# Attention before experts on one core: masks moved to TensorE, transposes two pairs ahead, banded heads first with one output tile per head, one v transfer, dummy matmuls

## Chip, cores and metric

The kernel runs on one core of one Trainium2 chip. The metric is the device time of one execution in microseconds (us), as the median over several executions. A "fast" execution is one within 1.5% of the fastest of its kernel; only those enter the ratios. The executions were spread over several chips, and the kernel before takes 277 to 282 us on the first of them and 267 to 271 us on the later ones, so kernels are compared by ratios or with runs beside them on the same chip.

## The reference

Four batches of attention with 8 heads, 768 positions and head size 64. Heads 0, 2 and 6 are causal ("retrieval"); heads 1, 3, 4, 5 and 7 are "streaming": they see the first 4 positions (the sinks) and the last 64. Every token then goes to one of 8 experts (two-layer networks, 512 to 1024 to 512), chosen by a given domain number.

```
scores = scale * q @ k.T
mask   = causal                                  for retrieval heads
mask   = causal & (pos < 4 | distance < 64)      for streaming heads
a      = softmax(where(mask, scores, -1e9));  x = a @ v     # all heads joined: 3072 x 512
out[domain == e] = relu(x[domain == e] @ w1[e]) @ w2[e]     # e = 0..7
```

## The kernel before

Work is in float16 with float32 sums in PSUM. For each batch and pair of heads, q and k are transposed on TensorE, copied out, multiplied into scores, passed through exp on ScalarE, and masked on VectorE by multiplying with 0 and 1. The product with v carries a column of ones (65 columns), which gives the softmax's denominator.

The masking on VectorE (cut):

```
# causal heads: after exp, the diagonal blocks are multiplied by the 0/1 mask
nc.vector.tensor_tensor(out=d, in0=d, in1=m_diag..., op=ALU.mult)
# streaming heads: the whole band is multiplied by the 0/1 mask
nc.vector.tensor_tensor(out=et, in0=et, in1=m_str..., op=ALU.mult)
```

The product with v of the streaming heads: one output tile holds all five heads of one block `it` of 128 positions; one sink product for all heads, 330 columns wide, and then ten band products, two for each head:

```
def part(it):                                   # six of these a batch
    ps = av_pool.tile([P, 5, VW], FP32, ...)
    if it > 0:
        nc.tensor.matmul(out=ps[all five heads],                  # 330 columns
            lhsT=eSink[b][0:96, P*(it-1) : P*it],                 # stationary 96 x 128
            rhs=vs_sink[0:96, b, :, :], start=True, stop=False)
    for h, s in SIDX.items():                                     # five heads
        for a in (2*it, 2*it + 1):
            nc.tensor.matmul(out=ps[hp : hp+64, s, 0 : D+1],
                lhsT=et[:, 64*a : 64*a + 64],                     # stationary 128 x 64
                rhs=rhs[:, 0 : D+1], ...)
    # ... normalize on VectorE, scatter the 128 rows to the experts' slots
```

After the last batch the kernel loads the tokens of expert 0 back (`load_x`), transposes them and runs the experts:

```
load_x(0); load_x(1)
x_transpose(0)
load_w(wB, 3)              # the fourth of the experts' weights
for e in range(E):
    layer1(e); ...; layer2(e); ...
```

The softmax here doesn't subtract the row's maximum and nothing guards it: scores larger than these inputs give would overflow.

## Time and profile before

| | before |
|---|---|
| median of 3 runs | 277.36 us (277.27 to 279.59) |
| profiled span | 275.1 us, granted TensorE clock 0.83 |
| attention: first scores to last matmul | 14.5 to 138.1 us |
| first expert matmul | 157.4 us |
| experts and output | to the end, TensorE full |

First the page of the profile: busy microseconds by engine with the share of the span, and the clock granted to TensorE in tenths of full speed in 40 equal slices of the span ("9" is 0.9 or more).

```profile
PE 196.7 (72%) x1979; PEld 109.9 (40%) x1979; DVE 120.9 (44%) x340; ACT 92.5 (34%) x109; POOL 120.8 (44%) x191
...
PEclk9999999655696558855955569999999999999995
```

Next the busy time of each engine by stretches of 15 us; the first columns are the stretch and its length, the last three the granted clock, the DMA share and GB/s.

```profile
core 0: us, PE busy (x) PEld busy (x) DVE busy (x) ACT busy (x) POOL busy (x), PEclk, DMA share, GB/s
...
75.00:90.00 15.00, 11.65 (x190) 7.11 (x190) 14.22 (x51) 9.31 (x11) 5.60 (x8) 0.81 1.53 169
...
120.00:135.00 15.00, 9.92 (x196) 7.19 (x190) 10.21 (x29) 5.45 (x7) 4.05 (x7) 0.60 0.11 37
135.00:150.00 15.00, 1.78 (x33) 1.00 (x33) 3.31 (x13) 0.00 (x0) 9.19 (x16) 0.63 0.46 102
```

The clock reads 9 in the first slices (before 46.6 us the trace has no record of it), but that is no measurement, and so the mean of 0.83 is too high: two causal score products of 448 columns take 0.56 us there at 42 us, and 0.36 us at 105 us, so TensorE ran cold early on. No engine is full in attention. In 75 to 90 us VectorE comes near it (14.22 of 15); from 135 to 150 hardly anything runs on TensorE. The list of waits says what TensorE stood still for: waiting instruction, the event that released it, us in total, times, longest.

```profile
engine line waited for: us in total, times, longest us
PE tpx_0_2304 L715 <- DMA xe_2297<-x_slots: 16.8, 1, 16.8
PE dom_ps L488 <- DVE r_dlow L484: 8.3, 1, 8.3
PE scs_2_0_453 L301 <- DVE kT_2_439 L218: 6.2, 1, 6.2
PE scs_2_0_946 L301 <- DVE kT_2_932 L218: 5.3, 1, 5.3
PE scs_2_0_1490 L301 <- DVE kT_2_1461 L218: 3.1, 1, 3.1
```

The largest wait is between attention and experts, for the tokens of expert 0 (`xe`). Many of the others are for VectorE, which copies the transposed k (`kT`) late because it is busy with masks. Last, the timeline of TensorE in one block of the streaming heads: start, duration, line, output and inputs, stationary tile (rows x columns), moving tile. Durations overlap, because matmuls are pipelined; the differences of the starts are what counts.

```profile
133.69 0.30 PE L419 MATMUL avs_1_2171<-vs_sink,eSk_2075 96*128 96x330 f16 x1 [0.43 <-DVE rcps_0_2163 L443]
133.92 0.22 PE L435 MATMUL avs_1_2171<-vsh_1793,eS_3_3_2015 128*64 128x65 f16 x1
133.92 0.22 PE L435 MATMUL avs_1_2171<-ve_1097,eS_3_3_2015 128*64 128x65 f16 x1
133.97 0.20 PE L435 MATMUL avs_1_2171<-vsh_1793,eS_3_2_1950 128*64 128x65 f16 x1
...
134.07 0.19 PE L435 MATMUL avs_1_2171<-ve_1097,eS_3_1903 128*64 128x65 f16 x1
134.35 0.31 PE L419 MATMUL avs_2_2191<-vs_sink,eSk_2075 96*128 96x330 f16 x1
```

### The profile page before, as it was taken

To read this page: it belongs to the slowest core of one execution; us is meant where nothing else is said; L and a number is where in the kernel's file an instruction comes from. 1 tells how busy PE (TensorE), PEld (TensorE's weight loads), DVE (VectorE), ACT (ScalarE), POOL (GpSimd) and SP (SyncE) were. 2 spreads that over 40 slices of the span, in tenths; PEclk is the share of its full clock that TensorE was granted. 3 is DMA by queue.
4 is the path that set the end of the run, shared out by engine and by line. 5 is a ranking of instruction groups with operands and counts; after the bars stand their busy time and mean duration, and the time that the engine had idled before them with its cause. 6 is when DMAs were issued, how large, how long until landed. Compare 5 with 4: busy or idle time off the path is not lost. (4 is left out here: it accounts for less than half of the span.)

```text
span 275.1 us, 4932 instructions
## 1 busy us (share of the span) xinstructions
PE 196.7 (72%) x1979; PEld 109.9 (40%) x1979; DVE 120.9 (44%) x340; ACT 92.5 (34%) x109; POOL 120.8 (44%) x191
## 2 busy tenths in 40 slices
PE   0279178783578478757600399999999999999940
PEld 0235045352344255444500245544554545454410
DVE  0835953874799654976720103141413141413120
ACT  1186067333585158625000032404150505051400
POOL 8579398584725840242464001535344440504140
PEclk9999999655696558855955569999999999999995
DMA  7999999957999549510119999899999998202030
GB/s 134 236 172 137 182 60 170 155 98 141 193 203 138 97 85 187 95 60 19 50 70 168 239 230 224 206 213 270 213 276 229 272 229 215 112 4 92 17 112 1
DMA packets 55731, 41.27 MB, mean 150 GB/s; under 512 B 27901, under 2 KB 49301, under 8 KB 55703
## 3 DMA queue, kind: packets, MB, share of 16 engines
q0 software_dynamic: 50096, 35.67, 78.9%
q1 hardware_dynamic: 5606, 5.24, 6.9%
q8 instruction: 16, 0.26, 0.4%
q14 instruction: 13, 0.10, 0.1%
HBM read 56.64 MB, written 11.53 MB: 248 GB/s over the span
## 5 line engine op out<-in xcount | busy, mean ns | idle before, releaser
L400 POOL DMA_INDIRECT x_slots<-xb_1111,dest_i x6 | 6.7, 1122 | 23.1 <-DVE xb_1111 L451 20.9
L177 POOL DMA_DIRECT2D ve_1097<-in_v_dram x12 | 9.0, 772 | 10.0 <-DMA w_0_943<-in_moe_w_dram 3.7
L715 PE MATMUL tpx_0_2304<-ct,xe_2297 128*128 128x128 f16 x8 | 1.0, 311 | 16.8 <-DMA xe_2297<-x_slots 16.8
L177 POOL DMA_DIRECT2D ve_159<-in_v_dram x12 | 9.3, 804 | 4.8 <-DMA k_156<-in_k_dram 3.1
L177 POOL DMA_DIRECT2D ve_141<-in_v_dram x12 | 9.0, 762 | 4.9 <-DMA q_131<-in_q_dram 2.6
L749 POOL DMA_INDIRECT out_dram<-ob_2404,idx_i x1 | 1.0, 1049 | 22.8 <-DVE ob_2404 L748 22.8
L742 ACT ACTIVATE hT_2329<-h_0_0_2330 128x896 f16<-128x896 f32 x1 | 0.9, 917 | 30.0 <-PE h_0_0_2330 L735 30.0
L177 POOL DMA_DIRECT2D ve_600<-in_v_dram x12 | 8.9, 772 | 4.4 <-DMA k_597<-in_k_dram 3.1
L400 POOL DMA_INDIRECT x_slots<-xb_1633,dest_i x6 | 5.8, 972 | 6.4 <-DVE rcps_1_2183 L443 3.4
L715 PEld LDWEIGHTS <-xe_2297 128*128 128x128 f16 (+1 forms) x16 | 1.4, 138 | 17.1 <-DMA xe_2297<-x_slots 16.9
L400 POOL DMA_INDIRECT x_slots<-xb_614,dest_i x6 | 6.5, 1083 | 3.0 <-DVE xb_614 L451 1.8
L400 POOL DMA_INDIRECT x_slots<-xb_245,dest_i x6 | 6.1, 1024 | 1.5 <-issue 1.1
L719 DVE COPY xT_2303<-tpx_0_2304 128x1024 f16<-128x1024 f16 x1 | 0.7, 691 | 13.4 <-PE tpx_0_2304 L715 13.4
L488 PE MATMUL dom_ps<-ct,r_dlow 24*128 24x24 f16 x1 | 0.2, 197 | 8.3 <-DVE r_dlow L484 8.3
L735 PEld LDWEIGHTS <-w_0_941 128*128 128x128 f16 x32 | 3.8, 119 | 5.4 <-issue 3.8
L301 PE MATMUL scs_2_0_453<-qT_2_388,kT_2_439 64*64 64x128 f16 (+2 forms) x12 | 0.5, 311 | 6.2 <-DVE kT_2_439 L218 6.2
L719 DVE COPY xT_2370<-tpx_0_2371 128x1024 f16<-128x1024 f16 x1 | 0.7, 692 | 9.3 <-PE tpx_0_2371 L715 9.3
L749 POOL DMA_INDIRECT out_dram<-ob_3152,idx_i x1 | 1.0, 971 | 7.8 <-DVE ob_3152 L748 7.8
L749 POOL DMA_INDIRECT out_dram<-ob_3021,idx_i x1 | 1.0, 971 | 7.7 <-DVE ob_3021 L748 7.7
L735 PEld LDWEIGHTS <-w_1_1485 128*128 128x128 f16 x32 | 3.1, 98 | 3.0
L735 PEld LDWEIGHTS <-w_5_2578 128*128 128x128 f16 x32 | 3.1, 98 | 3.0
L735 PEld LDWEIGHTS <-w_7_2831 128*128 128x128 f16 x32 | 3.1, 98 | 3.0
(875 smaller groups left out, 650.8 us busy)
## 6 DMA issues: line engine op xcount, KB each, us to landing
x_slots<-zt SPq DMA_DIRECT2D x8, 128.0 KB, 8.0
w_0_941<-in_moe_w_dram POOLq DMA_DIRECT2D x1, 1024.0 KB
w_0_943<-in_moe_w_dram POOLq DMA_DIRECT2D x1, 1024.0 KB
w_1_1485<-in_moe_w_dram POOLq DMA_DIRECT2D x1, 1024.0 KB
w_1_1487<-in_moe_w_dram POOLq DMA_DIRECT2D x1, 1024.0 KB
w_2_2271<-in_moe_w_dram POOLq DMA_DIRECT2D x1, 1024.0 KB
w_2_2273<-in_moe_w_dram POOLq DMA_DIRECT2D x1, 1024.0 KB
w_3_2325<-in_moe_w_dram POOLq DMA_DIRECT2D x1, 1024.0 KB
```

The source lines that it names most:

```text
L177: nc.gpsimd.dma_start(out=ves[b][:, t, 4 * par : 4 * par + 4, 0:D], in_=v[b, par::2, t * P : (t + 1) * P, :].rearrange("h p d -> p h d"),)
L301: yield lambda g=g, a0=a0, a1=a1, hp=hp: nc.tensor.matmul(out=dst[hp : hp + 64, a0 - c0 : a1 - c0], lhsT=kT[b, pi][rows, 64 * g : 64 * g + ...
L400: ins = nc.gpsimd.indirect_dma_start(out=xs_dram, out_offset=bass.IndirectOffsetOnAxis(ap=dest_i[:, t : t + 1], axis=0), in_=xbs[b][:, it, :],
L488: nc.tensor.transpose(out=dps[:], in_=dlow[:], identity=ident[0:NT, 0:NT])
L715: nc.tensor.transpose(out=ps[:, j, c, 0:n], in_=xe[e][0:n, g, c * P : (c + 1) * P], identity=ident[0:n, 0:n])
L719: nc.vector.tensor_copy(out=xT[e][:, :, 0:256].rearrange("p c (j n) -> p c j n", j=2), in_=ps[:].rearrange("p j c n -> p c j n"),)
L735: nc.tensor.matmul(out=sc[:, j, 0:CAP], lhsT=w1t[:, c, ft * P : (ft + 1) * P], rhs=xT[e][:, c, :], start=(c == 0), stop=(c == 3),)
L742: nc.scalar.activation(out=hT[e][:, 2 * fp : 2 * fp + 2, :], in_=sc[:, :, 0:CAP], func=AF.Relu)
L749: ins = nc.gpsimd.indirect_dma_start(out=out, out_offset=bass.IndirectOffsetOnAxis(ap=idx_i[:, col : col + 1], axis=0), in_=ob[:], in_offs ...
```

## The change

Its intent is to free VectorE, and to keep TensorE from waiting for it. The masks become additive and are matmuls with the identity, summed into the scores in PSUM before exp. The transposes of q and k run two head pairs ahead. The banded (streaming) pairs come first in a batch, and their products with v fill the gaps of the causal pairs. Each streaming head gets its own output tile for all six blocks, so that it can be normalized at once. v of a batch is one transfer. Dummy matmuls at the start and before the experts are to warm the clock. Parts of the routing arithmetic are rewritten. The core of the diff (cut, marked by "# ..."):

```diff
-PAIRS = [(0, 2), (6, 7), (1, 3), (4, 5)]
+PAIRS = [(1, 3), (4, 5), (6, 7), (0, 2)]
-    c16[:, 128:256] = pp[:, None] <= pp[None, :]
+    c16[:, 128:256] = np.where(pp[:, None] <= pp[None, :], 0.0, NEG)
# ... causal heads: score pieces are cut at the diagonal block, which gets a mask
+                mb = lambda c0=c0, c1=c1: nc.tensor.matmul(
+                    out=dst[:, c0 - p0 : c1 - p0], lhsT=ident, rhs=m_diag, start=False, stop=True
+                )
-            for J in range(NSO):
-                if 448 * c <= OFF[J] < 448 * c + 448:
-                    d = et[:, :, OFF[J] : OFF[J] + P]
-                    nc.vector.tensor_tensor(
-                        out=d, in0=d, in1=m_diag.unsqueeze(1).to_broadcast([P, 2, P]), op=ALU.mult
-                    )
# ... streaming heads: the mask is the first product of each half
+    def str_bias(c, dst):
+        nc.tensor.matmul(
+            out=dst[:, 0:384], lhsT=ident, rhs=m_str[:, 384 * c : 384 * c + 384], start=True, stop=False
+        )
# ... the product with v of the streaming heads: one tile for each head
-    def a_str_units(b):
-        def part(it):
-            # one sink product of 330 columns, then ten band products
+    def a_str_units(b, h):
+        def part(t0):
+            def f():
+                if t0 == 0:
+                    st["ps"] = av_pool.tile([P, NSO, VW], FP32, tag="av", name=f"avs_{b}_{h}")
+                for it in (t0, t0 + 1):
+                    if it > 0:
+                        nc.tensor.matmul(
+                            out=ps[:, it, 0 : D + 1],
+                            lhsT=eSink[b][0:96, P * (it - 1) : P * it],
+                            rhs=vs_sink[0:96, b, s, 0 : D + 1],
+                            start=True,
+                            stop=False,
+                        )
+                    for a in (2 * it, 2 * it + 1):
+                        kk = 64 if a == 0 else P
+                        nc.tensor.matmul(
+                            out=ps[hp : hp + 64, it, 0 : D + 1],
+                            lhsT=et[0:kk, 64 * a : 64 * a + 64],
+                            rhs=rhs[0:kk, 0 : D + 1],
+                            start=(it == 0),
+                            stop=True,
+                        )
+                if t0 == NSO - 2:
+                    normalize(b, h, ps)
# ...
+    def warm(n, name):
+        ps = sc_pool.tile([P, 2, 512], FP32, tag="sc", name=f"warm_{name}")
+        for i in range(n):
+            nc.tensor.matmul(out=ps[:, i % 2, :], lhsT=zt[:, 0:P], rhs=zt[:], start=True, stop=True)
# ... load_v: 12 transfers become one; scatters come after the last head of a batch
# ... stages of a batch: streaming pairs, sinks, causal pair, head 6; transposes two pairs ahead
     load_x(0)
     load_x(1)
+    warm(16, "moe")
     x_transpose(0)
     load_w(wB, 3)
```

The sink product was one for all heads of a block, and is now one for each head and block. In the order of the program it stands directly before that head's two band products: a stationary tile of 96 x 128, two of 128 x 64, again 96 x 128, and so on.

## The prediction

> **What bounds it now.** The busy table by stretches shows three parts of the 275.1 us span. Attention ends on TensorE at 138.1. Until the first expert matmul at 157.4 (timeline) nothing computes: scatters leave GpSimd until 143.8, the first x load is issued at 145.5, and TensorE waits 16.8 us for it (list of waits) while weights 2 and 3 share the DMA engines. Then the experts: TensorE busy 15.0 of every 15 us until 265, and the output tail.
>
> Attention takes 31 us a batch: first scores at 14.5, 42.4, 75.1, 105.2. TensorE is busy 86.3 of 127 us, VectorE 85.6, ScalarE 61.7. TensorE's waits on VectorE sum to about 30 us after the start: kT copies (6.2, 5.3, 3.1, 2.4, four of 1.9), mask products and normalizations. The gaps also cool the clock: granted clock 0.63 to 0.74; a 64x448 score matmul takes 550 ns in batches 0 and 1, 360 in 2 and 3. The Trainium skill ("TensorE: Matmul & The Clock Gate", Part 1) says that about 3.4 us of idling halves the clock; these pairs agree.
>
> **What the change does.**
> - Removes VectorE mask products: 6.4+4.1+8.9+2.2 = 21.6 us, some 8 us more of routing and kbd copies (3.9, to GpSimd).
> - Adds to TensorE per batch 18 masks of 128 columns, 10 of 384, about 15 cuts, 20 sink products: an estimate of 4 us, at the measured 50 to 60 ns per small matmul.
> - Transposes two pairs ahead take the 0.95 us kT copies out of TensorE's way: most of the 30 us of waits go, TensorE stays warm. Estimate: 20 to 23 us a batch.
> - Start: transposes at about 8 us instead of 10.9. But in batch 0 kbd copies sit behind the second v transfer in GpSimd's order, which waits until the first v has landed, near 25.5 (q and k of batch 1 land at 29.4 and 33.3). Stall of about 5 us at the sink scores, until 26 to 28.
> - One v transfer saves GpSimd 7 us a batch, off the path; rows stay 64 elements, so DMA time stays: 16 us a batch (q, k 3.9 each, v 8). With 11 to 12.5 us per expert's weights, loads up to weights 2 keep the DMA queue busy until about 110: nearly a second bound.
> - All six scatters now come after the last head, 1.28 us each: about 3 us more.
> - Dummy matmuls before the experts end long before x lands; the first expert still starts cold (572 ns matmuls). Worth about 0.
>
> **Sum.** Attention ends near 26.5 + 14 + 3x21.5 = 105 to 108 instead of 138. Normalization and scatters 9, load issue 1.6, x landing 7 to 9.5, transposes 2.5: first expert matmul near 129 instead of 157.4. Experts and tail unchanged (118 us). Gain 28 us.
>
> Predicted: **249 us**, 8 in 10 between 239 and 262. Faster by over 2%: 0.96; within: 0.02; slower: 0.02.
>
> **What shows each step.** First scores spaced 20 to 23 us from batch 1 on; TensorE's waits on VectorE in attention under 10 us; score matmuls of 360 ns from batch 1; a wait at batch 0's sink scores until 26 to 28; 19 to 23 us between attention's last matmul and the first expert's; expert stretch still full; first expert matmuls near 570 ns.
>
> **What would make it wrong.** The DMA queue is the bound: weights 2 delay the last scatters (255 to 262). TensorE, with more and smaller matmuls, needs 26 us a batch (262). Or x lands faster, with only weights 3 beside it, and the dummies bridge the gap (238).

## More of the kernel before

The five pairs of band products start within 0.15 us of each other, from 133.92 to 134.07. From the last pair to the next sink product it takes 0.28 us, of which TensorE is shown idle for 0.09.

## The result, and the profile after

| | before | changed |
|---|---|---|
| median, same chip | 278.48 us (277.27 to 282.2, 4 runs, the last one slow) | 296.98 us (295.82 to 297.72, 4 runs) |
| ratio of fast runs | | 1.068 (95%: 1.060 to 1.076) |
| profiled span, granted clock | 275.1 us, 0.83 | 294.9 us, 0.78 |
| attention's last matmul ends | 138.1 us | 154.4 us |
| first expert matmul | 157.4 us | 177.2 us |

A ratio is the mean time of one kernel's fast runs over that of the other's fast runs of the same rounds, so it is not quite the ratio of the medians quoted. The kernel became slower by about 7% where 10% faster was predicted. All of it lies before the experts: after the first expert matmul both kernels need 118 us.

The page of the changed kernel, the same lines as before:

```profile
PE 249.6 (85%) x2248; PEld 137.2 (47%) x2248; DVE 92.6 (31%) x208; ACT 93.2 (32%) x109; POOL 97.7 (33%) x167
...
PEclk9795555695559855596559556999999999999995
```

VectorE has lost 28 us of busy time, as intended. TensorE has gained 53, of which 36 in attention (122.2 against 85.8). The stretches show how full it is, and at what clock:

```profile
core 0: us, PE busy (x) PEld busy (x) DVE busy (x) ACT busy (x) POOL busy (x), PEclk, DMA share, GB/s
...
30.00:45.00 15.00, 15.00 (x128) 8.64 (x127) 3.87 (x11) 4.14 (x6) 1.52 (x1) 0.50 1.87 182
...
105.00:120.00 15.00, 15.00 (x143) 8.77 (x142) 5.31 (x20) 6.76 (x8) 0.36 (x2) 0.50 0.81 137
```

TensorE is shown busy for 15.00 of 15.00 us, and yet its granted clock is 0.50, as if it idled. VectorE is at 3.87 of 15. The list of waits confirms that TensorE no longer waits for VectorE:

```profile
PE tpx_0_2411 L724 <- DMA xe_2387<-x_slots: 16.2, 1, 16.2
PE sck_421 L364 <- POOL kbd L223: 7.4, 1, 7.4
PE tpk_0_183 L204 <- DMA k_132<-in_k_dram: 2.4, 1, 2.4
PE avs_4_1601 L442 <- DVE xb_1315 L383: 1.4, 1, 1.4
```

So the waits that the change was to remove are gone, and TensorE spends longer than before on what it executes. The timeline of one streaming head says on what:

```profile
29.89 0.23 PE L431 MATMUL avs_1_443<-vs_sink,eSk_420 96*128 96x65 f16 x1
30.05 0.26 PE L442 MATMUL avs_1_443<-vsh_429,eS_0_0_255 128*64 128x65 f16 x1
30.06 0.26 PE L442 MATMUL avs_1_443<-ve_141,eS_0_0_255 128*64 128x65 f16 x1
30.25 0.23 PE L431 MATMUL avs_1_443<-vs_sink,eSk_420 96*128 96x65 f16 x1
30.41 0.26 PE L442 MATMUL avs_1_443<-vsh_429,eS_0_0_255 128*64 128x65 f16 x1
30.42 0.26 PE L442 MATMUL avs_1_443<-ve_141,eS_0_0_255 128*64 128x65 f16 x1
30.61 0.23 PE L431 MATMUL avs_1_443<-vs_sink,eSk_420 96*128 96x65 f16 x1
```

A group of three small products (the sink product and two band products) takes 0.36 us, from 29.89 to 30.25 and from 30.25 to 30.61, at a clock near 0.50. Elsewhere, at a higher clock (64 to 66 us), it still takes 0.29 us. The two band products start 0.01 us apart. The time passes between the tile of 128 columns and the tiles of 64 columns, in both directions. No line shows a wait (a wait would stand in brackets). Together the sink and band products keep TensorE busy for 43.2 us in the changed kernel, against 16.6 us before (overlaps counted once).

The Trainium skill has a sentence for this. The page "TensorEngine Tiling (Array Packing)", section "Key Properties" under "Tiling Modes", says that changing the tiling mode, "not just tile", drains TensorE. It gives no cost. The modes that the page lists are tile sizes: 128 x 128, 128 x 64, 64 x 128 and so on. Here the mode is taken to be the size class of the stationary tile, which the probe below bears out. Counting the changes of this class along the matmul records of attention, one by one, gives 173 before and 411 in the changed kernel (96 rows counted as 128, which the probe below justifies).

**Theory A.** Every change of tiling mode costs a fixed drain. The change adds more than 200 of them, mostly by alternating sink and band products, some by the mask matmuls. If the array does no work while it drains, the clock falls too, though the profile shows TensorE busy.

**Rival B.** The sink product and the band products sum into the same PSUM words directly after one another, and the accumulation waits for the write. The number of switches would then not matter, and writing other words in between would help.

**Other rivals.** The mask matmuls alone cost it; or the dummy matmuls do.

### The profile page after: what moved, and what is told of

Its sections match the earlier page's. It is cut to its first block, busy times and chain, and to the rows that moved or that the text cites. A ratio compares the mean times of both kernels' runs of the same rounds, so it can differ in the third digit from the quotient of the medians.

```text
span 294.9 us, 5270 instructions
## 1 busy us (share of the span) xinstructions
PE 249.6 (85%) x2248; PEld 137.2 (47%) x2248; DVE 92.6 (31%) x208; ACT 93.2 (32%) x109; POOL 97.7 (33%) x167
## 5 line engine op out<-in xcount | busy, mean ns | idle before, releaser
L457 POOL DMA_INDIRECT x_slots<-xb_1847,dest_i x6 | 6.0, 1000 | 17.7 <-DVE xb_1847 L383 16.5
L252 PEld LDWEIGHTS <-ct 128*128 128x128 f16 x72 | 5.6, 106 | 11.6 <-issue 10.7
L758 POOL DMA_INDIRECT out_dram<-ob_2511,idx_i x1 | 1.1, 1054 | 25.0 <-DVE ob_2511 L757 25.0
L364 PE MATMUL sck_421<-qT_0_181,kbd 128*32 128x320 f16 x2 | 0.9, 448 | 7.4 <-POOL kbd L223 7.4
L457 POOL DMA_INDIRECT x_slots<-xb_254,dest_i x6 | 6.4, 1071 | 2.2 <-DVE r_olo L495 1.3
L728 DVE COPY xT_2410<-tpx_0_2411 128x1024 f16<-128x1024 f16 x1 | 0.7, 693 | 20.5 <-PE tpx_0_2411 L724 20.5
L457 POOL DMA_INDIRECT x_slots<-xb_1315,dest_i x6 | 6.0, 1003 | 2.1 <-DVE xb_1315 L383 1.2
L457 POOL DMA_INDIRECT x_slots<-xb_748,dest_i x6 | 6.0, 1002 | 2.1 <-DVE xb_748 L383 1.2
L744 PEld LDWEIGHTS <-w_0_1201 128*128 128x128 f16 x32 | 3.8, 120 | 5.6 <-issue 4.3
L481 PEld LDWEIGHTS <-zt 128*128 128x128 f16 x29 | 3.3, 122 | 6.0 <-issue 3.4
L223 POOL COPY kbd<-kT_0_638 64x4 f16<-64x4 f16 x2 | 0.4, 212 | 16.9 <-DVE kT_0_638 L217 16.9
L481 PE MATMUL warm_start<-zt 128*128 128x512 f16 x10 | 4.2, 600 | 1.3 <-DVE zt L623 1.3
L223 POOL COPY kbd<-kT_0_1756 64x4 f16<-64x4 f16 x2 | 0.4, 182 | 13.0 <-DVE kT_0_1756 L217 12.9
L364 PEld LDWEIGHTS <-kbd 128*32 128x32 f16 x24 | 0.7, 96 | 8.3 <-POOL kbd L223 8.0
L744 PEld LDWEIGHTS <-w_5_2685 128*128 128x128 f16 x32 | 3.1, 98 | 3.0
L744 PEld LDWEIGHTS <-w_7_2938 128*128 128x128 f16 x32 | 3.1, 98 | 3.0
L744 PEld LDWEIGHTS <-w_1_1660 128*128 128x128 f16 x32 | 3.1, 98 | 3.0
L744 PEld LDWEIGHTS <-w_3_2432 128*128 128x128 f16 x32 | 3.1, 98 | 3.0
L744 PEld LDWEIGHTS <-w_2_2001 128*128 128x128 f16 x32 | 3.0, 98 | 3.2 <-issue 0.4
```

Source lines behind the costliest of these rows:

```text
L223: nc.gpsimd.tensor_copy(out=kbd[r, b % 2, g, 4 * hh : 4 * hh + 4], in_=dst[r, 0:4])
L252: mb = lambda c0=c0, c1=c1: nc.tensor.matmul(out=dst[:, c0 - p0 : c1 - p0], lhsT=ident, rhs=m_diag, start=False, stop=True)
L364: nc.tensor.matmul(out=sc[32 * g : 32 * g + 32, c, 0:320], lhsT=kbd[:, b % 2, g, :], rhs=qT[b, PAIRS.index(pr)][:, P + 320 * c : P + 320 * ...
L457: ins = nc.gpsimd.indirect_dma_start(out=xs_dram, out_offset=bass.IndirectOffsetOnAxis(ap=dest_i[:, t : t + 1], axis=0), in_=xbs[b][:, it, :],
L481: nc.tensor.matmul(out=ps[:, i % 2, :], lhsT=zt[:, 0:P], rhs=zt[:], start=True, stop=True)
L728: nc.vector.tensor_copy(out=xT[e][:, :, 0:256].rearrange("p c (j n) -> p c j n", j=2), in_=ps[:].rearrange("p j c n -> p c j n"),)
```

## The experiments

### One pattern at a time: probe

This kernel computes nothing of the reference and gives a wrong result (it writes zeros). It runs bursts of 65-column products after a stretch of large matmuls that warm the clock: tiles of 128 columns only; pairs of 64-column tiles only; the two alternating on the same PSUM words, then on other words; grouped by fives; two halves in place of the full tile; 64 rows against 128; and 96 rows against 128.

```diff
+    def p_alt_same(ps, rows=96, shift=0):      # shift=3: other PSUM words
+        for i in range(60):
+            full(ps, (i + shift) % 6, rows=rows, start=(i == 0))
+            for hp in (0, 64):
+                half(ps, i % 6, hp, stop=(i == n - 1))
```

> A kernel of matmul patterns alone (wrong result on purpose), 60 groups each of 65 columns, after a burst that keeps the clock at full rate. Theory A: only 128-column tiles, 50 to 60 ns a matmul; only pairs of 64-column tiles, 60 to 70 ns a pair; 128-column matmul and pair in turn, 280 to 300 ns a group, the same with 96 or 128 rows and whether the pair adds to the same words or to others; with the 128-column matmul cut in two halves, under 150 ns a group; five and five, under 170 ns a group. Theory B: in turn but to other words, under 170 ns a group; halves, still near 280.

The windows of the probe, one for each pattern (60 repetitions each): 128 columns only; pairs only; alternating, its first 5.5 us; the rest of it; grouped by fives; 96 against 128 rows.

```profile
core 0: us, PE busy (x) PEld busy (x) DVE busy (x) POOL busy (x), PEclk, DMA share, GB/s
20.16:21.98 1.82, 1.82 (x62) 1.82 (x61) 0.00 (x0) 0.00 (x0) 1.00 0.03 9
27.25:29.27 2.02, 2.02 (x121) 1.98 (x121) 0.00 (x0) 0.00 (x0) 1.00 0.04 8
34.46:40.00 5.54, 5.54 (x59) 3.89 (x57) 0.00 (x0) 0.00 (x0) 0.99 0.01 3
40.00:54.66 14.66, 14.66 (x123) 9.36 (x123) 0.00 (x0) 0.00 (x0) 0.50 0.00 1
...
128.34:134.77 6.43, 6.43 (x181) 5.30 (x180) 0.00 (x0) 0.00 (x0) 1.00 0.01 3
...
165.82:169.72 3.90, 3.90 (x121) 3.90 (x120) 0.00 (x0) 0.00 (x0) 1.00 0.00 0
```

A full tile alone takes 30 ns (1.82 us over 60), a pair alone 34 ns (2.02 over 60), so a group of both without a switch would take 64 ns. Alternating at clock 0.99, the full tiles start 287 ns apart in the trace. Each group has two switches, so one switch costs (287 - 64) / 2, or about 111 ns. Grouped by fives, 60 groups with 24 switches took 6.43 us, 107 ns a group: (107 - 64) x 60 / 24 = 108 ns a switch. The two patterns agree; 0.108 us is used below. After the clock has fallen to 0.50 a group takes 360 ns. If the 64 ns of work double there to 128, a switch takes 116 ns: its length hardly depends on the clock.

Other results of the same run: alternating on other PSUM words took 340 ns a group over the whole burst, on the same words 337 (287 and 360 ns at the two clocks in both), so Rival B is refuted here. With two halves in place of the full tile a group took 82 ns, a burst with no switch (with a gap of 0.70 us at its issue). A tile of 64 rows against one of 128, both with 128 columns, took 309 ns a couple (at a mean clock of 0.65; 270 at full clock), so rows are part of the mode. Rows of 96 against 128 took 65 ns a couple (3.90 us over 60), so these are one mode.

The other half of the theory is in the third and fourth lines. The pattern is the same, TensorE is shown busy all the time, and the clock falls from 0.99 to 0.50 after 5.5 us. It fell in each of the four bursts that alternate shapes (one of them with a full tile of 128 rows), 4.0 to 5.6 us after their start, and in none of the others. Three of these lasted under 4 us, but the one by fives lasted 6.4. The Trainium skill ("TensorE: Matmul & The Clock Gate", Part 1) says that the gate follows how busy the array has been over windows of about 3.4 us. That agrees only if drains count as idle, which no view of the profile shows as such.

### Fewer switches, other switches: e1_hoist, e2_stagger, e3_dvemasks

The first computes the five sink products of a head first, then its band products. The switches fall, and the products remain.

```diff
+                # ... sink(i) is the sink product of block i; start and stop flags are moved to match
+                if t0 == 0:
+                    for i in range(1, NSO):
+                        sink(i)
                 for it in (t0, t0 + 1):
-                    if it > 0:
-                        nc.tensor.matmul(...)      # the sink product of this block
```

> The changed kernel, with the five sink products of each banded head issued first and its banded products after them; same number of matmuls, same operands. Theory A (the array loses about 0.1 to 0.15 us at each change between 128-column and 64-column stationary tiles): 8 changes fewer per head, 160 in all, so a head's products fall from 1.7 to 2.2 us to about 1 us, and the kernel from 297 to 272 to 280 us. Theory B (a matmul that adds to the PSUM words just written must wait for that write): much the same gain, since the distance grows too. Theory C (the added mask matmuls are the cause): within 1% of the changed kernel.

Measured: 259.7 us, ratio 0.962 (0.954 to 0.970). By moving 100 small products the kernel went from slower to faster than the one before. Expected were 272 to 280 us. Against the changed kernel on a chip like this one (294.59 us, below) it gained 35 us, of which 176 fewer switches make 19; the granted clock in attention rose besides, from 0.61 to 0.79.

The second issues the sink product of the next block before the bands of this one. It has nearly as many switches as the changed kernel (383 against 411), but the products that follow one another write other PSUM words.

```diff
                 # ... sink(i) and the flags as above
                 for it in (t0, t0 + 1):
-                    if it > 0:
-                        nc.tensor.matmul(...)      # the sink product of this block
+                    if it + 1 < NSO:
+                        sink(it + 1)
```

> The changed kernel, with the sink product of block it+1 issued just before the banded products of block it: as many changes between 128- and 64-column tiles as before, but never two matmuls in a row into the same PSUM words. Theory A: within 1% of the changed kernel (297 us), 0.29 to 0.36 us per block still. Theory B: as fast as the run with the sinks hoisted (272 to 280 us).

Measured: 292.06 us, ratio 1.081 (1.071 to 1.091). It is as slow as the changed kernel, within 0.9% (294.59 us on a like chip, below). Rival B falls in the kernel as well as in the probe.

The third puts all masks back on VectorE as 0/1 products after exp, and leaves the alternation.

```diff
-                mb = lambda c0=c0, c1=c1: nc.tensor.matmul(out=..., lhsT=ident, rhs=m_diag, ...)
+                    nc.vector.tensor_tensor(out=d, in0=d, in1=m_diag..., op=ALU.mult)
     # ... the mask tables hold 0 and 1 again; streaming heads:
-            str_bias(c, sc[:, 0, :])
+            nc.vector.tensor_tensor(out=et, in0=et, in1=m_str..., op=ALU.mult)
```

> The changed kernel with the masks as products on VectorE again, everything else kept. Theory A: about 90 changes of the tile shape fewer and 72 + 40 mask matmuls fewer, 12 to 18 us of TensorE time, of which waits on VectorE give back a few: 280 to 288 us. Theory C (the masks are the whole cause): 265 us or less.

Measured: 283.28 us, ratio 1.052 (1.043 to 1.061). The masks on TensorE cost something here (11 us against the changed kernel's 294.59), but taking them away leaves the kernel slower than before. They are not the main cause.

### The alternation alone, in the kernel before: b1_alternate

Only the sink product of the kernel before is split into one for each head, each directly before its band products. Masks, transposes and order stay.

```diff
-                if it > 0:
-                    nc.tensor.matmul(out=ps[all five heads], ..., rhs=vs_sink[0:96, b, :, :], ...)
                 for h, s in SIDX.items():
+                    if it > 0:
+                        nc.tensor.matmul(out=ps[:, s, :], ..., rhs=vs_sink[0:96, b, s, :], ...)
```

> The kernel before, with only this part of the change: the sink product of a block, one matmul of 330 columns for five heads, becomes five of 65 columns, each just before the banded products of its head. 80 matmuls more; 160 changes more between 128- and 64-column tiles. Theory A, with 0.11 us per change as the matmul patterns showed: 17 us, and a few more by a cooler clock: 6 to 9% slower than the kernel before. If only the count of matmuls matters (30 to 60 ns each): 1 to 2% slower.

Measured: 283.75 us against 268.82 for the kernel before beside it, ratio 1.059 (1.050 to 1.067). That is 15 us for 160 switches (333 against 173 in the traces) and 80 small products more. At 0.108 us a switch alone 17 us were to be expected if every one lay on the critical path.

### The sink product in two halves: e5_halves, e6_halves_k128

Here the order stays as the change has it, and only the shape changes. The sink product is cut into two with 64 columns each. That is 100 products more, and no switch between sinks and bands.

```diff
                     if it > 0:
-                        nc.tensor.matmul(out=ps[:, it, 0 : D + 1],
-                            lhsT=eSink[b][0:96, P * (it - 1) : P * it], ...)
+                        for hp in (0, 64):
+                            nc.tensor.matmul(out=ps[hp : hp + 64, it, 0 : D + 1],
+                                lhsT=eSink[b][0:96, P * (it - 1) + hp : P * (it - 1) + hp + 64], ...)
```

> The changed kernel, with each sink product cut into two 64-column halves in its old place, between the banded products: 100 matmuls more than the changed kernel, and no change of tile shape between sinks and bands. Theory A: as fast as the run with hoisted sinks (0.96 of the kernel before) or up to 1% faster. If the count of matmuls, or writes to the same words, were the cause: slower than the changed kernel (over 1.07).

Measured: 261.77 us (one of four runs slow), ratio 0.972 (0.960 to 0.985). That is faster than the kernel before, but whether by 2% is unclear. With 100 products more than the changed kernel it is far below its ratio of 1.07 to 1.09, so neither the number of products nor the writes to the same words are the cause.

The next also lets the first band product of each head contract 128 rows rather than 64 (the added rows contribute zeros), so no switch is left between the products with v of a head.

```diff
-                        kk = 64 if a == 0 else P
+                        kk = P
```

> The same, and the first band product of a head contracts over 128 rows (the added rows are zero) instead of 64, so that a head has no change of shape at all: 40 changes fewer. Theory A: 4 to 5 us faster than the run with halves alone, about 0.945 of the kernel before.

Measured: 248.01 us (two of four runs slow; the fast ones took 245.5 and 246.46), ratio 0.925 (0.913 to 0.936); it beats both kernels. The timeline shows the same work as the three lines of the changed kernel's groups, now in one mode:

```profile
55.62 0.19 PE L443 MATMUL avs<-vsh,eS 128*64 128x65 f16 x1
55.62 0.19 PE L443 MATMUL avs<-ve,eS 128*64 128x65 f16 x1
55.65 0.20 PE L432 MATMUL avs<-vs_sink,eSk 96*64 96x65 f16 x2
55.69 0.20 PE L443 MATMUL avs<-vsh,eS 128*64 128x65 f16 x1
```

A group of two sink halves and two bands now takes 0.07 us (from 55.62 to 55.69), where three products took 0.29 to 0.36. The sink scores of the four batches start at 26.7, 48.2, 70.9 and 91.2 us, 20 to 23 us apart, which is the spacing that the prediction gave for the changed kernel.

From the one edit to the other 32 switches go (223 to 191 in the traces; 40 were expected), about 3.5 us, but the time falls by 14. The windows of attention explain it, from the first sink scores to the last matmul (columns as above). First the halves alone:

```profile
26.80:117.20 90.40, 86.73 (x1470) 54.45 (x1471) 49.02 (x120) 54.78 (x67) 36.49 (x66) 0.77 1.07 147
```

Then the halves with 128 rows:

```profile
26.70:104.00 77.30, 72.82 (x1506) 47.34 (x1507) 49.10 (x122) 55.58 (x67) 36.49 (x66) 0.95 1.27 175
```

And the changed kernel:

```profile
27.10:154.40 127.30, 122.21 (x1406) 73.72 (x1407) 49.61 (x122) 55.70 (x67) 36.83 (x66) 0.63 0.85 117
```

The granted clock is 0.77, 0.95 and 0.63. An account in two terms, an estimate worked out from the traces, fits these five kernels: the length of a drain is fixed, and the rest of the busy time is work that stretches with the clock. The work at full clock is then clock x (busy - switches x 0.108 us).

| kernel | switches | clock | PE busy, us | of it drains, us | work at full clock, us |
|---|---|---|---|---|---|
| changed | 411 | 0.63 | 122.2 | 44.4 | 49.0 |
| e2_stagger | 383 | 0.61 | 120.2 | 41.4 | 48.1 |
| e1_hoist | 235 | 0.79 | 86.7 | 25.4 | 48.4 |
| e5_halves | 223 | 0.77 | 86.7 | 24.1 | 48.2 |
| e6_halves_k128 | 191 | 0.95 | 72.8 | 20.6 | 49.6 |

The work comes out the same within 2 us, as it should, since these kernels do almost the same products; without the term for drains, clock x busy would range from 67 to 77 us. From the changed kernel to the one with halves and 128 rows, attention becomes 50.0 us shorter. Of that, 220 fewer switches give 23.8 us directly. The clock gives about 26 us (49.0 / 0.63 = 77.8 against 49.6 / 0.95 = 52.2). So about half of the loss is the drains, and the other half is the lower clock. That drains lower the clock is shown by the probe for alternation alone; in the kernels it is the reading that fits, and the number of switches doesn't settle the clock alone (0.77 with 223, 0.95 with 191).

### Dummy matmuls and the same chip: e4_nowarm, a2_changed_again

```diff
-    warm(10, "start")
     run_t(t_units(0, 0))
-    warm(3, "t1")
# ...
-    warm(16, "moe")
```

> The changed kernel without its three groups of dummy matmuls. Recorded view (they are worth about nothing): within 1% of the changed kernel, 1.06 to 1.075 of the kernel before. If they do warm the clock for what follows: 1 to 2% slower than the changed kernel.

Measured: 295.61 us, ratio 1.103 (1.094 to 1.112). The ratio differs from the changed kernel's 1.068, but so does the chip. So the changed kernel was run once more, unedited, on a chip where the kernel before takes the same 268.8 us.

> The changed kernel, unedited, on this chip, so that runs without the dummy matmuls can be compared with it at home. The kernel before took 277 to 282 us on the first chip and 267 to 271 us on the chips of the later runs. If the changed kernel scales with the chip, 286 to 289 us and a ratio near 1.07; if its time is set by mode switches that do not scale, 294 to 298 us and a ratio near 1.10, like the run without dummies (295.6 us, 1.103).

Measured: 294.59 us, ratio 1.094 (1.085 to 1.103). The changed kernel takes 295 to 297 us on either chip, while the kernel before gains 10 us from one to the other; why was not studied. The intervals of the two ratios overlap, so the dummy matmuls are worth nothing that these runs can tell.

### On from the best: c2d_halves_dvediag, e7_w3late, e8_halves_k128_nowarm

All three are edits of the kernel with halves and 128 rows. They ran on another chip than it, where the kernel before takes the same 268.8 us. The first puts only the diagonal masks of the causal heads back on VectorE, for fewer switches around the mask matmuls:

```diff
     # ... c16 holds 0 and 1 for the diagonal blocks again; pieces are no longer cut there
-                mb = lambda c0=c0, c1=c1: nc.tensor.matmul(out=..., lhsT=ident, rhs=m_diag, ...)
+                    nc.vector.tensor_tensor(out=d, in0=d, in1=m_diag..., op=ALU.mult)
```

> The halves-and-128-rows kernel (248.0 us, ratio 0.925) with only the diagonal masks of the causal blocks back on VectorE, so about 70 fewer mode switches around mask matmuls. Theory A (about 0.11 us a switch): attention 5 to 8 us shorter, 240 to 244 us, ratio 0.90 to 0.91, if VectorE has the room. Rival: TensorE waits on the VectorE masks give it back: 247 to 252 us, ratio 0.92 to 0.935.

Measured: 249.77 us, ratio 0.929 (0.920 to 0.938). The expected gain did not come. The time is the one that the rival gave, but TensorE's waits for the masks that it names come to 0.3 us in the list of waits. The window of attention:

```profile
26.70:107.60 80.90, 73.42 (x1386) 47.43 (x1387) 57.97 (x170) 54.93 (x67) 36.82 (x66) 0.77 1.24 173
```

There are 128 switches rather than 191, but the clock was 0.77, not 0.95: it stood at 0.50 until 43 us, from 53 to 60 and again from 94 us on. TensorE idled for 7.5 us of the window (80.90 - 73.42) against 4.5. Between the sink scores of the third and the fourth batch, where both kernels were granted the full clock, it needed 19.3 us against 20.3, so the fewer switches do pay there. That the added idling lets the clock fall is not shown. The clock also differs between executions: in the next two runs, which leave attention as it was, it was 0.92 and 0.88 there.

The second loads the fourth expert's weights later, so that they do not share the DMA with the tokens:

```diff
     x_transpose(0)
-    load_w(wB, 3)
# ...
         layer2(e)
+        if e == 0:
+            load_w(wB, 3)
```

> The halves-and-128-rows kernel with the third weights loaded only after the first expert's second layer, so that they do not share the DMA with the scatters and the load of x between attention and experts. If contention makes x land late (9.8 us from issue in the changed kernel), x lands in 4 to 6 us, the first expert matmul comes 3 to 5 us sooner, 243 to 245 us, ratio 0.905 to 0.915. Rival (the landing is latency of the transfer itself): 247 to 249 us, ratio 0.92 to 0.93.

Measured: 240.48 us, ratio 0.895 (0.886 to 0.904), the fastest. The timeline of the load and of the first use of the tokens, first without this edit (SPq is the queue that issues the load):

```profile
115.54 0.38 SPq L705 DMA_DIRECT2D xe<-x_slots  x1
...
124.69 1.78 PE L725 MATMUL tpx<-ct,xe 128*128 128x128 f16 x16 [17.26 <-DMA xe<-x_slots]
```

and with it:

```profile
115.67 0.38 SPq L705 DMA_DIRECT2D xe<-x_slots  x1
...
118.71 1.78 PE L725 MATMUL tpx<-ct,xe 128*128 128x128 f16 x16 [10.49 <-DMA xe<-x_slots]
```

The tokens are there 3.0 us after the issue rather than 9.2. The gain was larger than the expected 3 to 5 us: 6.0 us earlier in the timeline, and 5.9 us between the means of the fast runs (240.05 against 245.98 us).

The third removes the dummy matmuls from the kernel with halves and 128 rows.

> The halves-and-128-rows kernel without the dummy matmuls. The prediction on record held the dummies to be worth about 0: 247 to 249 us, ratio 0.92 to 0.93. Rival (with the attention fast, the dummies at the start warm the clock for the first projections or those at the end for the first expert): 250 to 253 us, ratio 0.935 to 0.945.

Measured: 249.5 us, ratio 0.924 (0.915 to 0.934), against 0.925 with them. They are worth nothing here either.

## Why the prediction was wrong

**The step that failed** is "Adds to TensorE per batch 18 masks of 128 columns, 10 of 384, about 15 cuts, 20 sink products: an estimate of 4 us, at the measured 50 to 60 ns per small matmul". It priced the added matmuls by their number. The measured price comes from blocks in which the tile shape does not change. What the change adds is an order in which it changes at almost every step, from 173 switches to 411, at 0.108 us each. The sink and band products alone grew from 16.6 to 43.2 us over the four batches, 6.6 us a batch where 4 were allowed for all additions. Splitting the sink product in the kernel before, and nothing else, cost 15 us; grouping the products by shape took the changed kernel from about 295 to 259.7 us.

**The step that failed with it** is "TensorE stays warm" (that is, keeps its full clock). It took for granted that a TensorE that doesn't wait is warm. In the changed kernel TensorE is shown busy for 122 of 127 us of attention, and its mean granted clock is 0.63. Its 64x448 score products took 0.53 to 0.55 us in every batch, where 0.36 from batch 1 on was predicted. The probe shows alternation alone taking the clock from 0.99 to 0.50. Nor does the trace of the kernel before show that a fall takes 3.4 us of idling, as the prediction had it from the page: in the 7 us before the clock fell at 50.0, 84.2 and 114.9 us, TensorE's longest idle stretch was 1.5 us.

**The spacing of the batches**, "20 to 23 us", was therefore wrong for the changed kernel: its sink scores are at 27.1, 61.6, 95.3 and 130.1 us, 34 to 35 us apart. These three spacings are 38.5 us longer than the 64.5 in the prediction's sum, and the last batch took 24.3 us from its sink scores on rather than 14: this is the whole delay of attention. The spacing is right for the kernel with the switches inside the heads removed (20 to 23 us; 248.0 us measured, on a chip with a faster kernel before).

**What held.** TensorE's waits for VectorE in attention are under 10 us in all, the largest 1.4 us. The first sink scores wait until 27.1 us (predicted 26 to 28), for the copies that stand behind the second v transfer. From the last matmul of attention to the first of the experts it takes 22.8 us (predicted 19 to 23). The experts' stretch is unchanged, and the first expert still starts cold. The dummy matmuls are worth nothing that these runs can tell. VectorE was relieved as computed.

**What the warning list had.** "TensorE, with more and smaller matmuls, needs 26 us a batch (262)" named the right engine and still gave it 8 us a batch too few, again because it thought of the number of products and not of their order. The remark that the tokens would land faster beside fewer weights was right in kind: with weights 3 out of the way they landed in 3.0 us. The dummies did not bridge that gap, though.

**What stays open.** What fills the 0.11 us of a switch: "drain" is the word for it here, but no run separates an emptying array from a weight load that can't start earlier. Why the clock falls in some executions and not in others (halves alone against halves with 128 rows; the diagonal masks on VectorE), and why the kernel before is 10 us faster on some chips and the changed one isn't.

## What to carry to other kernels

Count the changes of the stationary tile's shape class along TensorE's program order, not only the matmuls: at 0.108 us each, a switch cost here as much as three small products of 30 to 34 ns. Before an order that interleaves shapes is adopted, make the shapes equal (cut the wide tile in two, pad the contraction with zeros) or group by shape; both turned a loss of some 7 to 9% into a gain. Read the granted clock beside the busy share: busy for 15.00 of 15.00 us at a clock of 0.50 was the sign here of time lost that no list of waits shows.

## What the Trainium skill lacked or had wrong

- "TensorEngine Tiling (Array Packing)", Key Properties: it says that a mode switch drains TensorE and gives no cost. Measured: 0.108 to 0.111 us a switch at full clock, 0.116 (an estimate) at half. It also doesn't say that the profile shows this time as busy.
- The same page gives row and column tiling for sizes of up to 64, but doesn't say which mode a tile between the listed sizes runs in. Here 96 and 128 rows with 128 columns shared one (65 ns for two products); 64 and 128 rows did not (270 ns for two), nor 64 and 128 columns (287 ns for three).
- "TensorE: Matmul & The Clock Gate", Part 1: it explains the gate by how busy TensorE was, and its two cases of an oscillating clock are waits for DMA and cycling through PSUM. Switching modes cools it as well: alternating shapes took the granted clock from 0.99 to 0.50 after 5.5 us with TensorE shown busy throughout.
- "Trainium Kernel Development and Optimization", the passage on reading a trace: it rightly calls matmul busy time a bad metric, and names MFU (the share of peak arithmetic, not worked out here) and the weight loads' busy share as the good ones for judging how close a kernel is to its peak. The latter didn't tell the kernels apart here: 58% of attention in the changed kernel (73.72 of 127.30 us) against 61% (47.34 of 77.30) in one whose attention is 50 us shorter. The granted clock did, with 0.63 against 0.95.
- "TensorE: Matmul & The Clock Gate", Part 1, warns that a profile's clock events can be unreliable, but not that they may be missing at the start. In the kernel before the clock reads 1.00 up to 46.6 us, where its first record stands, while two 64x448 score products take 0.56 us at 42 us against 0.36 us at 105 us.
